# One of three output groups padded, scaling and decay powers open to GpSimd, the last output rows in two banks and two queues, and a new instruction table

## The chip, the core and the metric

The kernel runs on one core of a Trainium2 chip. The metric is the device time of one execution in microseconds (us). The core's engines work at the same time and wait for one another through semaphores: TensorE (PE in the rows, its weight loads PEld), VectorE (DVE), ScalarE (ACT), GpSimd (POOL), and SyncE (SP), which issues the DMA transfers.

## What is computed

```
# attention: r, k, v (4, 8, 768, 48); w, u (8, 48)
for t in range(S):
    cur = einsum('bhd,bhe->bhde', u * kt, vt)
    y[:, :, t] = einsum('bhd,bhde->bhe', rt, state + cur)
    state = w * state + einsum('bhd,bhe->bhde', kt, vt)
# x (4, 768, 384): the eight heads side by side
h = maximum(x @ w_in, 0)                      # w_in (384, 1024)
conv = sum over k of conv_w[k] * h shifted by k - 1 along the sequence
out = (h * sigmoid(conv)) @ w_out             # w_out (1024, 384)
```

All inputs and the output are 32-bit floats, but the three FFN weights arrive as 64-bit floats, read as pairs of 32-bit words, and are converted on the chip.

## The kernel before

The sequence of 768 is cut into groups of 128 positions (two chunks of 64), six to a batch, 24 in all. The recurrence is done by chunks, for four pairs of heads at a time, the two heads of a pair on the upper and the lower half of the partitions. For each group `prep` (L366) loads K and R into KR and scales them by powers of the decay (line L198 in the rows, written `KR<-KR,TKR`), makes a token-major K (`kt`, for groups 0 to 3 on TensorE at L381), the diagonal QQ (`q`, L393) and spreads QQ into RS (L410, L415 or L418). TensorE then computes scores (`VA`, into psA), additions to the state (`VU`, into psU) and outputs (`VY`, into psY). `chain` (L492) masks the scores into RS with a predicated copy (L496) and carries the state: it fades the old state into SD (L489, on ScalarE L487) and adds the new one into SS (L510, L515). For groups 0, 1 and 2 the visits VA, VU and VY are apart and borrow idle banks; from group 3 on one visit `V` holds the scores and additions of one group and the outputs of the one before.

`split` (L519) brings an output into XT as a rounded part (ScalarE, L527) and a remainder (VectorE, L528). The FFN wants the 384 features as three blocks of 128 partitions, while four pairs of heads give four blocks of 96 used partitions. Two ways lead there. In a padded group (`g < PAD`, before: groups 0, 1 and 2) TensorE writes the fourth pair's features, in three parts of 16, directly under the other three pairs: this needs a copy of the fourth pair's V (VP, L405) and of its state (SPP, L503), and more matmuls. In the other groups all four pairs are written apart, and six DMA transfers from XT to XT (L539) move the fourth pair's rows, once for each half of a batch.

The FFN works on eight units of three groups (382 or 386 columns) and on eight blocks f of 128 hidden features. `first` (L542) does nine matmuls into one of two HP banks (L559) and the chain relu (L566), taps (L567, L570, L570), sigmoid (L573), gate (L574) and the split of the result into GH (L576) and GL (L198). `second` (L581) does three matmuls (L591) for each of the three output blocks m = 0, 1, 2 into PO0 to PO2; after f = 7 ScalarE scales PO into OS (L598) and SyncE stores it. The weights come in 16 pieces into three ST buffers (`convert`, L326 to L353).

Nothing is scheduled at run time: the functions number their operations as they are called, and the table ORDER (L42) lists the numbers in the order in which each engine gets them. A suffix a, d or p picks ScalarE, VectorE or GpSimd for an operation marked "any". SyncE has one queue, in that order, so that a transfer that waits holds back all behind it.

Of the kernel before, what the change touches and what calls it, by code (L numbers as in the profile page):

```python
# [37 lines left out]
LEAD, EARLY, APART, PAD = 5, NEED[0], 4, NEED[0]  # L38
# [4 lines left out]
28 17 0 8 12 15 10 1 16 4 21 14 9 5 29 11 20 2 23 18 22 45 13 26 35 37 19 3 33 46 39 34 52 36 57 84 40 58 83 30  # L43
41 66 31 61d 42 43 38 74 59 6 32 75 62 78d 47 79 48a 54d 60a 49 210 76 209 50 63 7 51d 86a 67 53 65d 85 80 64a
87 232 82p 216 90 68 69 231 70a 55 44 77d 56 71p 105 92 212a 72 106 88 211 94d 109d 238 91 213 102 93 214 110
73a 89d 217 215d 107 95 111 81a 218d 112p 234a 97d 278 114 219 108a 279 113d 233 115 100 128 98 235 96a 99p 220
129 117 239 221p 285 116 118a 240d 126 101 301 24 236 25 119 241 300 280 281d 127 133 120a 242 282 121a 243d
237d 142 157d 123 125 283 160d 103 132 151 122 152 136p 124 104 134 148 150 287a 149 286 158d 200 303a 325 288
302 284d 307 135a 304 289 326 222 155 201 131 156 202 130 305 203 332 137 306p 223 204 154 224 140 159 144p 138
205 225 290p 139a 141 206 226 177p 269 145 172 175 153 227 146a 178p 228 143 270 291 161p 271 147 179 309a 272  # L50
229 162 164p 308 273 328a 371 310 274 176 171 292 275 327 207 230d 377 316 293 329 173 334a 208d 370 168 165 294
333 166p 170 315 169 276 180p 395 314 317 167 174 311 163 313 184p 318 339 295 277p 330 182 319 296 181a 331p
320 297 335 338 191 312d 321 361 195d 258 372 322 198p 189 186 183 190 373a 340 185 196p 379a 433 187 386 298
188 193 378 362 194 396 363 299d 244 387 380 336 374 388 364 337p 375 389 384 249 257 376p 365 385 381 259 250
# [97 lines left out]
def rwkv_ffn_kernel(tc, krd, krt, vt, wd, ut, w_in, conv_w, w_out, out):  # L152
# [4 lines left out]
    with ExitStack() as ctx:  # L157
# [24 lines left out]
        def act(n):  # L182
            return 0.093 + n / 1200.0
# [538 lines left out]
```

## Time and profile before

| what | value |
| --- | --- |
| time, median of 3 runs | 295.63 us (295.6 to 296.38) |
| the profiled execution | 296.4 us, of it 294.5 us span |
| TensorE busy | 281.9 us (96%) |
| VectorE, ScalarE, GpSimd busy | 245.8, 199.4, 102.4 us |
| weighted TensorE clock | 0.988 of 2.4 GHz |
| DMA moved | 37.48 MB |

The span runs from the first to the last instruction of the profiled execution; 1.9 us of its time lie outside. A busy share is an average over the whole span; what a stage waits for is read in that stage.

### The profile page before, as it was taken

To read this page: it belongs to the slowest core of one execution; us is meant where nothing else is said; L and a number is where in the kernel's file an instruction comes from. 1 tells how busy PE (TensorE), PEld (TensorE's weight loads), DVE (VectorE), ACT (ScalarE), POOL (GpSimd) and SP (SyncE) were. 2 spreads that over 40 slices of the span, in tenths; PEclk is the share of its full clock that TensorE was granted. 3 is DMA by queue.
4 is the path that set the end of the run, shared out by engine and by line. 5 is a ranking of instruction groups with operands and counts; after the bars stand their busy time and mean duration, and the time that the engine had idled before them with its cause. 6 is when DMAs were issued, how large, how long until landed. Compare 5 with 4: busy or idle time off the path is not lost.

```text
span 294.5 us, 10667 instructions
## 1 busy us (share of the span) xinstructions
PE 281.9 (96%) x4484; PEld 268.9 (91%) x4484; DVE 245.8 (83%) x469; ACT 199.4 (68%) x495; POOL 102.4 (35%) x134
## 2 busy tenths in 40 slices
PE   8798997899999999999999999999999999999995
PEld 3798886799999999999989999999999999999995
DVE  5889898989989799999988889989987866665771
ACT  4449798889886687764584568855665666567662
POOL 4121284353774722436384224334250014011100
PEclk9869999999999999999999999999999999999999
DMA  6969998695245664557266155561631002200202
GB/s 178 235 196 243 232 230 208 165 246 130 77 138 172 145 171 131 185 146 202 57 181 192 33 134 133 158 149 34 161 83 57 0 2 63 61 0 0 82 0 81
DMA packets 18499, 37.48 MB, mean 127 GB/s; under 512 B 3538, under 2 KB 11156, under 8 KB 18452
## 3 DMA queue, kind: packets, MB, share of 16 engines
q1 hardware_dynamic: 18452, 36.81, 47.1%
q8 instruction: 35, 0.57, 0.9%
q14 instruction: 12, 0.10, 0.1%
HBM read 30.01 MB, written 4.72 MB: 118 GB/s over the span
## 4 chain that ended last, share of the span: by engine, by line
PE 86%; DMA 6%; issue 2%; DVE 2%; POOL 1%; ACT 1%; SPq 0%; POOLq 0%
PE PO L591 35%; PE HP L559 33%; PE psY L479 9%; DMA ST<-in_w_in_dram 4%; PE psA L479 3%; PE psU L479 3%; DMA KR<-in_krd_dram 2%; PE PO L263 1%; PE HP L479 1%; PE PO L393 1%; POOL GL L198 1%; DVE KR L198 1%; SPq L202 0%; DVE KP L198 0%; ACT CC L336 0%
## 5 line engine op out<-in xcount | busy, mean ns | idle before, releaser
L559 PE MATMUL HP<-XT,wi 128*128 128x384 f32 (+1 forms) x576 | 111.7, 341 | 2.4 <-DVE GL L198 1.7
L591 PE MATMUL PO<-GH,wo 128*128 128x386 f32 (+1 forms) x384 | 109.8, 342 | 0.2 <-issue 0.2
L559 PEld LDWEIGHTS HP<-XT,wi 128*128 128x128 f32 x576 | 101.8, 188 | 3.6 <-DVE GL L198 1.8
L570 DVE SCALAR_TENSOR_TENSOR CV<-HP,cw,CV 128x382 f32<-128x382 f32 (+1 forms) x128 | 78.1, 614 | 16.9 <-ACT CV L567 15.2
L591 PEld LDWEIGHTS PO<-GH,wo 128*128 128x128 f32 x384 | 70.8, 189 | 1.6 <-issue 0.4
L591 PE MATMUL PO<-GL,wo 128*128 128x382 f32 (+1 forms) x192 | 65.1, 339 | 0.1
L198 POOL TENSOR_TENSOR GL<-SG,GH 128x382 fp32r<-128x382 f32 (+1 forms) x27 | 27.5, 1019 | 84.2 <-ACT GH L576 78.2
L566 ACT ACTIVATE HP<-HP 128x384 f32<-128x384 f32 (+1 forms) x64 | 30.6, 478 | 31.3 <-PE HP L559 30.9
L573 ACT ACTIVATE SG<-CV 128x382 f32<-128x382 f32 (+1 forms) x64 | 33.5, 524 | 26.1 <-DVE CV L570 25.5
L574 DVE TENSOR_TENSOR SG<-HP,SG 128x382 f32<-128x382 f32 (+1 forms) x64 | 35.4, 553 | 12.2 <-ACT SG L573 11.4
L479 PE MATMUL psY<-RS,KV 64*48 64x64 f32 x720 | 43.8, 221 | 1.3 <-issue 1.3
L479 PE MATMUL psY<-KR,SS 48*48 48x64 f32 x660 | 40.4, 216 | 0.5 <-issue 0.5
L576 ACT CAST GH<-SG 128x382 fp32r<-128x382 f32 (+1 forms) x64 | 32.5, 509 | 10.0 <-DVE SG L574 9.7
L567 ACT ACTIVATE CV<-HP,cw 128x382 f32<-128x382 f32 (+1 forms) x64 | 37.2, 581 | 1.4
L591 PEld LDWEIGHTS PO<-GL,wo 128*128 128x128 f32 x192 | 36.2, 189 | 0.4 <-POOL GL L198 0.4
L479 PEld LDWEIGHTS psY<-RS,KV 64*48 64x48 f32 x720 | 32.5, 121 | 1.6 <-issue 1.4
L198 DVE TENSOR_TENSOR KR<-KR,TKR 112x512 f32<-112x512 f32 x48 | 32.6, 691 | 0.8 <-DMA KR<-in_krd_dram 0.5
L479 PEld LDWEIGHTS psY<-KR,SS 48*48 48x48 f32 x660 | 30.8, 120 | 0.6 <-issue 0.6
L479 PEld LDWEIGHTS psA<-KR 48*64 48x64 f32 x704 | 22.3, 135 | 5.0 <-issue 3.2
L479 PE MATMUL psA<-KR 48*64 48x64 f32 x704 | 25.2, 221 | 0.0
L198 DVE TENSOR_TENSOR GL<-SG,GH 128x386 fp32r<-128x386 f32 (+1 forms) x37 | 20.5, 556 | 4.0 <-ACT GH L576 3.9
L479 PE MATMUL psU<-KV 64*48 64x48 f32 x672 | 20.1, 208 | 1.9 <-issue 1.8
(113 smaller groups left out, 347.4 us busy)
## 6 DMA issues: line engine op xcount, KB each, us to landing
KR<-in_krd_dram SPq DMA_DIRECT2D x24, 448.0 KB, 5.2
KV<-in_krt_dram SPq DMA_DIRECT2D x40, 192.0 KB, 3.7
KV<-in_vt_dram SPq DMA_DIRECT2D x48, 96.0 KB, 3.5
ST<-in_w_in_dram SPq DMA_DIRECT2D x16, 192.0 KB, 4.9
ST<-in_w_out_dram SPq DMA_DIRECT2D x8, 384.0 KB, 7.0
out_dram<-OS SPq DMA_DIRECT2D x12, 193.0 KB, 2.1
out_dram<-OS SPq DMA_DIRECT2D x12, 191.0 KB, 2.2
XT<-XT SPq DMA_DIRECT2D x42, 48.0 KB, 2.8
```

The lines of the kernel that those rows point to most:

```text
L198: op(eng, d, rd, wr, lambda e: e.tensor_tensor(**kw), cls, port=True)
L263: PE.matmul((psY, psU, HP[1], PO[0], PO[2])[min(k, 4)], wz[:, :128], wz, start=True, stop=True)
L393: PE.matmul(qb[o:o + 64, n:n + 1], kp[o:o + 48, p, t], uw[o:o + 48, p:p + 1], start=True, stop=True)
L479: PE.matmul(y, a, b_, start=s0, stop=s1)
L559: PE.matmul(hp, wi[a][:, j, fs], X[:, x, j, t], start=(j == 0 and k == 0), stop=(j == 2 and k == 2))
L566: op("act", 0.093 + n / 1200.0, [], [H_], lambda e: A.activation(hp, hp, AF.Relu, scale=1.0 / WS))
L567: op("act", 0.158 + n / 1200.0, [H_, "cw"], [("T", ti)], lambda e: A.activation(t1, hp[:, 1:n + 1], AF.Copy, scale=cw[:, 3 * f + 1:3 * f + ...
L570: op("dve", 0.117 + n * 1.085e-3, [H_, "cw"], [("T", ti)], lambda e, k=k: V.scalar_tensor_tensor(out=t1, in0=hp[:, k:n + k], scalar=cw[:, ...
L573: op("act", 0.11 + n / 1200.0, [("T", ti), "sgt"], [("SG", ti)], lambda e: A.activation(sg, t1, AF.Sigmoid))
L574: op("dve", dps(n), [H_], [("SG", ti)], lambda e: V.tensor_tensor(out=sg, in0=hp[:, 1:n + 1], in1=sg, op=ALU.mult), "GG")
L576: op("act", act(n), [("SG", ti)], [("GH", gi)], lambda e: A.copy(gh, sg))
L591: PE.matmul(PO[m][:, :n], wo[a][:, f, ms], g2[x], start=(f == 0 and k == 0), stop=(f == NF - 1 and k == 2))
```

## The change

Only group 2 is padded (`PADS = (2,)`). Groups 0 and 1 write their fourth pair apart, and six more XT to XT transfers, of 256 columns, move it after group 1's split; the first `first` reads what they bring. Their VP and SPP copies go, and the zeros for VP1 and SPP1 are written later. The scaling of K and R, the higher decay powers (PW2) and the diagonal decay matrix DW may go to GpSimd: of the 48 scalings 25 go there. In the last unit the output block m = 2 is summed as 192 columns in PO2 and 194 in psY, for all eight f; the output copies may go to VectorE (10 of 25 do), and the last store is issued by ScalarE's queue. A matmul of 256 columns on zeros (an `f` in the table) is put once between the first small matmuls. The table is new as a whole, so that engines and places change throughout.

```diff
@@ the constants @@
-LEAD, EARLY, APART, PAD = 5, NEED[0], 4, NEED[0]
+LEAD, EARLY, APART = 5, NEED[0], 4
+PADS = (2,)
@@ ORDER: the whole table is new; its first and its last line @@
-28 17 0 8 12 15 10 1 16 4 21 14 9 5 29 11 20 2 23 18 22 45 13 26 35 37 19 3 33 46 39 34 52 36 57 84 40 58 83 30
...
-1468 1453 1464 1472 1454d 1465 1471 1466d 1475 1482 1474 1483 1479 1484 1473 1480 1476 1481 1477 1478
+28 27 0 8 25 24 11 10 1 18 12 4 9 45 29 46 5 35 33 37p 79 52 17 36 20 2 39 19 58d 34 80 30 38p 57d 40 42 32 f
...
+1494a 1495
@@ powers2 @@
-            grow(32, 32)
-            grow(64, 31)
+            for n, m in ((32, 32), (64, 31)):
+                e.tensor_tensor(out=PW[:, :, n + 1:n + m + 1], in0=PW[:, :, 1:m + 1],
+                                in1=PW[:, :, n:n + 1].broadcast_to([112, NP, m]), op=ALU.mult)
@@ PW2 and DW @@
-        op("dve", 0.55, ["PW"], ["PW2"], powers2)
-        op("dve", 0.25, ["PW", "PW2", "ident"], ["DW"], lambda e: V.tensor_tensor(
+        op("any", {"dve": 0.55, "pool": 0.85}, ["PW"], ["PW2"], powers2, port=True)
+        op("any", {"dve": 0.25, "pool": 0.55}, ["PW", "PW2", "ident"], ["DW"], lambda e: e.tensor_tensor(
@@ prep @@
-                tt("dve", 512, ks, [(key, i)], "KR", out=v, in0=v, in1=W.unsqueeze(2).broadcast_to([112, NP, 2, C]), op=ALU.mult)
+                tt("any", 512, ks, [(key, i)], "KR", out=v, in0=v, in1=W.unsqueeze(2).broadcast_to([112, NP, 2, C]), op=ALU.mult)
...
-            if g < PAD:
+            if g in PADS:
@@ outputs @@
-                for p in range(3 if g < PAD else NP):
+                for p in range(3 if g in PADS else NP):
-                        if g < PAD:
+                        if g in PADS:
-                        if g < PAD and inter:
+                        if g in PADS and inter:
-                        mms.append((ps[64 - o:112 - o, m:m + C], KV[i][o:o + 64, 2, p, c, :], RS[j][o:o + 64, 2 * p + c, :], g >= PAD, not inter))
+                        mms.append((ps[64 - o:112 - o, m:m + C], KV[i][o:o + 64, 2, p, c, :], RS[j][o:o + 64, 2 * p + c, :], g not in PADS, not inter))
-            if g < PAD:
+            if g in PADS:
@@ chain @@
-                if g + (1 - c) < PAD:
+                if g + (1 - c) in PADS:
@@ split @@
-            r, np_ = (128, 3) if g < PAD else (112, NP)
+            r, np_ = (128, 3) if g in PADS else (112, NP)
-            if gi + 1 not in cuts or g < PAD:
+            if g in PADS or gi + 1 not in cuts and g + 1 not in PADS:
-            h = cuts.index(gi + 1) - 1
+            h = sum(c <= gi for c in cuts) - 1
@@ second @@
-            for m in range(NM):
-                ms = slice(m * 128, m * 128 + 128)
-
-                def mm(e, m=m, ms=ms):
+            h = n // 4 * 2
+            for m, x0, x1, bank, key in ((0, 0, n, PO[0], "o0"), (1, 0, n, PO[1], "o1")) + (
+                    ((2, 0, n, PO[2], "o2"),) if u < NU - 1 else ((2, 0, h, PO[2], "o2"), (2, h, n, psY, "psY"))):
+                ms, w_ = slice(m * 128, m * 128 + 128), x1 - x0
+
+                def mm(e, m=m, ms=ms, x0=x0, x1=x1, bank=bank):
-                        PE.matmul(PO[m][:, :n], wo[a][:, f, ms], g2[x], start=(f == 0 and k == 0),
+                        PE.matmul(bank[:, :x1 - x0], wo[a][:, f, ms], g2[x][:, x0:x1], start=(f == 0 and k == 0),
-                op("pe", 3 * n * 0.459e-3, [("wo", 0, f), ("wo", 1, f), ("GH", gi), ("GL", gi)], [f"o{m}"], mm, "f2", 3 * n)
+                op("pe", 3 * w_ * 0.459e-3, [("wo", 0, f), ("wo", 1, f), ("GH", gi), ("GL", gi)], [key], mm, "f2", 3 * w_)
-                    o = OS[q][:, :n]
-                    op("act", act(n), [f"o{m}"], [("OS", q)], lambda e, m=m, o=o: A.activation(
-                        o, PO[m][:, :n], AF.Copy, scale=1.0 / WS))
-                    dma([("OS", q)], [("out", u, m)], out[ms, b * S + t0:b * S + t0 + n], o, 128, 4 * n, cls="out")
+                    o = OS[q][:, :w_]
+
+                    def store(e, bank=bank, o=o, w_=w_):
+                        if e is A:
+                            A.activation(o, bank[:, :w_], AF.Copy, scale=1.0 / WS)
+                        else:
+                            V.tensor_scalar(out=o, in0=bank[:, :w_], scalar1=1.0 / WS, scalar2=None, op0=ALU.mult)
+                    op("any", {"act": act(w_), "dve": dps(w_)}, [key], [("OS", q)], lambda e, st=store: st(e))
+                    last = key == "psY"
+                    dma([("OS", q)], [("out", u, m, x0)], out[ms, b * S + t0 + x0:b * S + t0 + x1], o, 128, 4 * w_,
+                        0.6 if last else 0.52, cls="out", eng="act" if last else "sp")
```

TensorE, groups 0 and 1 (matmuls grouped as in the program; HP_108, HP_109, PO_110, PO_111 are the borrowed banks HP0, HP1, PO0, PO1, and KV_64 to KV_66 the buffers of groups 0 to 2). Before:

```order
L479 MATMUL psU<-KV_64 48x48 x16
L479 MATMUL HP_108<-KR_62 64x64 x16
L479 MATMUL psY<-RS_67,VP_120 64x64 x2
L479 MATMUL psY<-RS_67,KV_64 48x64 x2
...
L479 MATMUL HP_109<-KV_65 48x48 x16
L393 MATMUL PO_111<-uw,KP_117 64x1 x16
L381 MATMUL psU<-DW,KR_63 64x48 x16
L479 MATMUL PO_111<-KR_63 64x64 x16
L479 MATMUL psU<-KV_66 48x48 x16
L479 MATMUL PO_110<-RS_68,VP_121 64x64 x2
L479 MATMUL PO_110<-KR_62,SPP_123 64x64 x2
```

The same place with the change:

```order
L483 MATMUL psU<-KV_64 48x48 x16
L483 MATMUL HP_108<-KR_62 64x64 x16
L483 MATMUL HP_109<-KV_65 48x48 x16
L483 MATMUL psY<-RS_67,KV_64 48x64 x10
L483 MATMUL psY<-KR_61,SS_71 48x64 x2
...
L385 MATMUL psU<-DW,KR_63 64x48 x16
L397 MATMUL PO_111<-uw,KP_117 64x1 x16
L483 MATMUL PO_110<-RS_68,KV_65 48x64 x2
L483 MATMUL PO_110<-KR_62,SS_72 48x64 x2
...
L483 MATMUL PO_111<-KR_63 64x64 x16
L483 MATMUL psU<-KV_66 48x48 x16
```

Group 0's output (into psY) now stands behind group 1's additions (HP_109) and has lost its VP and SPP matmuls; group 1's output (into PO_110) has lost them too and stands ahead of group 2's scores and additions instead of behind them.

SyncE, the transfers around the reload of the K and R buffers (KR_61, KR_62, KR_63) and of the stores' new place. Before:

```order
L202 DMA KR_61<-in_krd_dram 112x1024
L202 DMA ST_97<-in_w_in_dram 64x768 x2
L202 DMA KV_65<-in_krt_dram 64x768 x2
L202 DMA ST_98<-in_w_out_dram 128x768
L202 DMA uu<-in_ut_dram 64x192
L202 DMA ST_96<-in_w_in_dram 64x768 x2
L202 DMA uu<-in_ut_dram 64x192
L202 DMA KR_62<-in_krd_dram 112x1024
L202 DMA KV_64<-in_vt_dram 64x384
```

With the change:

```order
L205 DMA KR_61<-in_krd_dram 112x1024
L205 DMA KV_64<-in_vt_dram 64x384
L205 DMA ST_96<-in_w_in_dram 64x768 x2
L205 DMA ST_97<-in_w_in_dram 64x768 x2
L205 DMA ST_98<-in_w_out_dram 128x768
L205 DMA XT_75<-XT_75 16x2x256 x6
L205 DMA KR_62<-in_krd_dram 112x1024
L205 DMA KV_64<-in_vt_dram 64x384
L205 DMA ST_96<-in_w_out_dram 128x768
```

Six transfers of XT to XT, which wait for group 1's split, now stand ahead of group 4's K and R (KR_62) and of the second half of group 3's V (KV_64).

## Rows read from the trace of the kernel before

**Rows 1.** The page's head and its first part (span, busy time of each engine), and the row of its third part on the fetching of instructions (packets, MB, share of the 16 DMA engines).
```profile
span 294.5 us, 10667 instructions
PE 281.9 (96%) x4484; PEld 268.9 (91%) x4484; DVE 245.8 (83%) x469; ACT 199.4 (68%) x495; POOL 102.4 (35%) x134
q8 instruction: 35, 0.57, 0.9%
```

**Rows 2.** Busy time by stretch: from and to in us, the length, then for PE, PEld (weight loads), DVE, ACT and POOL the busy us and the instructions, then TensorE's granted clock as a share of 2.4 GHz, the DMA share, GB/s.
```profile
14.00:16.00 2.00, 0.79 (x19) 0.78 (x20) 2.00 (x4) 0.00 (x0) 0.93 (x2) 0.50 0.82 227
18.00:20.00 2.00, 2.00 (x48) 2.00 (x46) 2.00 (x6) 0.72 (x3) 0.00 (x0) 0.58 0.44 111
...
60.00:100.00 40.00, 40.00 (x642) 38.65 (x633) 36.92 (x70) 32.38 (x89) 25.71 (x30) 1.00 0.58 156
100.00:140.00 40.00, 39.67 (x772) 37.58 (x771) 37.98 (x71) 28.43 (x76) 15.48 (x19) 1.00 0.57 157
140.00:180.00 40.00, 39.53 (x671) 38.12 (x670) 35.54 (x68) 25.37 (x61) 15.94 (x17) 1.00 0.40 111
```

**Rows 3.** The same view, cut at TensorE's four longest gaps: the four stretches of work, and the first and the last of the gaps, which lie between them (columns as in rows 2).
```profile
0.00:13.46 13.46, 11.92 (x221) 8.22 (x222) 9.54 (x25) 6.18 (x17) 3.60 (x19) 0.98 0.84 205
13.46:15.21 1.75, 0.00 (x1) 0.00 (x0) 1.72 (x4) 0.00 (x0) 1.47 (x2) 0.50 0.73 205
15.21:27.50 12.29, 12.29 (x382) 12.20 (x381) 10.43 (x23) 8.12 (x25) 2.59 (x6) 0.82 0.78 216
...
28.59:45.65 17.06, 15.85 (x381) 14.52 (x381) 15.92 (x33) 14.48 (x40) 8.21 (x9) 1.00 0.99 227
...
47.36:53.20 5.84, 5.83 (x126) 5.49 (x127) 5.06 (x11) 5.02 (x16) 3.96 (x5) 1.00 0.90 224
53.20:54.49 1.29, 0.00 (x0) 0.00 (x0) 1.28 (x4) 0.99 (x3) 0.58 (x1) 1.00 0.82 221
```

**Rows 4.** TensorE in order of time: start, us, line, operation, output and inputs, shapes, how many, and in brackets the idle time before and what ended it. Of group 0's and group 1's outputs and the first FFN matmuls.
```profile
19.17 0.42 PE L479 MATMUL psY<-KR,SS 48*48 48x64 f32 x4
19.39 0.42 PE L479 MATMUL psY<-RS,VP 64*64 64x64 f32 x4
...
24.35 0.27 PE L479 MATMUL PO<-RS,VP 64*64 64x64 f32 x2
...
26.01 0.28 PE L479 MATMUL PO<-RS,KV 64*48 64x64 f32 x4
26.13 0.28 PE L479 MATMUL PO<-KR,SS 48*48 48x64 f32 x4
...
32.82 3.41 PE L559 MATMUL HP<-XT,wi 128*128 128x384 f32 x18
39.48 1.85 PE L559 MATMUL HP<-XT,wi 128*128 128x384 f32 x9 [0.52 <-DVE SG L574]
```

**Rows 5.** VectorE and ScalarE in order of time (columns as in rows 4), before 50 us: the predicated copy into RS, the two halves of a split into XT, and ScalarE's forms of the diagonal and of the fading.
```profile
19.35 0.73 DVE L496 COPY_PREDICATED RS<-mask,HP 128x512 f32<-128x512 int32 x1
47.82 0.68 DVE L528 TENSOR_TENSOR XT<-psY,XT 112x512 fp32r<-112x512 f32 x1
46.99 0.57 ACT L527 CAST XT<-psY 112x512 fp32r<-112x512 f32 x1
38.44 2.00 ACT L415 ACTIVATE RS<-eye,QQ 128x64 f32<-128x64 f32 x8
40.77 1.00 ACT L487 ACTIVATE SD<-SS,PW 112x48 f32<-112x48 f32 x4
```

**Rows 6.** SyncE's stores from XT to XT (the moves between partitions): issue time in ns min/median/max and how many, then us from issue to landing, over the whole span; and how long the loads issued from 26 to 32 us took to land (how many, KB each, median us).
```profile
L202 SPq DMA_DIRECT2D XT<-XT x42: 585/614/1759, 62.7 to 251.4; - x42
DMA to landing us min/median/max: 2.1/2.8/5.4
KV<-in_vt_dram SPq DMA_DIRECT2D x2, 96.0 KB, 6.1
uu<-in_ut_dram SPq DMA_DIRECT2D x1, 48.0 KB, 5.0
```

**Rows 7.** GpSimd's and VectorE's groups by line and shape: how many | busy us, mean ns of one | idle before them; and in order of time a row of GpSimd, and two of the same operation on VectorE, the second of which lies over GpSimd's.
```profile
L198 POOL TENSOR_TENSOR KP<-KR 112x512 f32<-112x512 f32 x1 | 1.3, 1285 | 5.4 <-DVE KR L198 5.4
L198 DVE TENSOR_TENSOR KR<-KR,TKR 112x512 f32<-112x512 f32 x48 | 32.6, 691 | 0.8 <-DMA KR<-in_krd_dram 0.5
77.56 1.02 POOL L198 TENSOR_TENSOR KV<-KV 128x384 f32<-128x384 f32 x1
21.77 0.35 DVE L489 TENSOR_TENSOR SD<-SS,PW 112x192 f32<-112x192 f32 x1
77.10 1.70 DVE L489 TENSOR_TENSOR SD<-SS,PW 112x192 f32<-112x192 f32 x1
```

**Rows 8.** The end, in order of time (columns as in rows 4), and the page's row on the landing of output stores.
```profile
285.87 0.34 PE L591 MATMUL PO<-GL,wo 128*128 128x386 f32 x1
286.41 0.34 PE L591 MATMUL PO<-GL,wo 128*128 128x386 f32 x1
...
290.84 0.34 PE L591 MATMUL PO<-GH,wo 128*128 128x386 f32 x1
291.22 0.49 ACT L598 ACTIVATE OS<-PO 128x386 f32<-128x386 f32 x1 [0.57 <-PE PO L591]
out_dram<-OS SPq DMA_DIRECT2D x12, 193.0 KB, 2.1
```

More of the change, by code (lines that the diff above doesn't have):

```diff
@@ new lines @@
+495 508 450 511 496 407a 349 420p 497 509a 405 451p 498 512 499 421p 513 506a 514 523 462 413 423p 515 411 414
+406 516 419p 483 521 408 417 517 409a 522 507 422 418p 555 503a 410 412 524 518 463d 525 520 500 467 526 556
+501p 527 557 469d 528 488p 558 533 473 481 470 534 559 519p 482 471a 532 474 484 564 489p 560 529 485 566 561
+545 530 567 472 424a 510 490 491d 478 531d 416 565 486d 475 562 577 550p 568 479 563d 607 569 544 578 492a 468
+477 597 551p 570 476 571 480 576 553d 598 504 608 487d 599 606 549d 572 619 600 592p 618 573 535 552 537p 601
@@ new lines @@
+702d 695 723 731 712 706 696p 703 743 711 707 732 675 704p 724 644 714p 705 725 753 774 726 733 645 741 719d 734
+754 773 713d 727 764 701 728p 735 746p 736 775 757p 765 759d 785 737 766 744 767 762p 738 768 776 747 815 769
+758d 739 752 748d 740p 755 770 787 749 816 777 745 786 771 821p 756 778 797 669 750 788 760p 779 780 772d 799
+802d 789 820p 841 781 761 798 790 751 838 763p 791 835 782 800 792 842d 793 824d 783 794 784p 826 803 814 795
+804d 806 796p 836d 844 805 827 807 819p 828 801 813 870a 829 853 877 883p 855 845 830 868 846 822d 831 823 832
@@ new lines @@
+969a 967 1043 984p 979 959 1006 983 971 960 950p 1000 1007a 972 1003 961 1051p 1001a 1009 962d 992 993 970 985p
+994 1018 1010 1049d 1020 1011 1032 995 1033 1012 996 1035a 997 1050 998 1013 1030 1086 999p 1021 1014 982 1039
+1015 1045 990p 1040 976 1062 1036 1022 1041 1037d 1053 1004a 1047p 977 1023 1038 1044 1034 1079a 1087 1064 1046d
+978 1054 1019 1024 1055 1031 1002 1025 975 1063 1052d 1026 1077 1008 1016 1027 974 1017p 1056 1028 973 1057
+1092p 1065 1029d 1083 1089 1058 1088 1059 1148 1093p 1075 1084 1066 1085 1074 1080 1149 1067 1154d 1106 1081a
@@ new lines @@
+1068 1076 1090d 1108 1060 1094 1097 1061p 1069 1078 1070 1091p 1095d 1107 1098 1118 1099 1082 1120 1152p 1100
+1133 1101 1071 1102 1103 1109 1147 1096d 1104 1005 1072 1135d 1105p 1211d 1121 1110 1073d 1111 1112 1132 1122
+1113 1119 1139 1134 1209p 1130 1123 1131 1114 1124 1174 1115 1155p 1168 1136 1116 1125 1171 1137p 1159 1126
+1117p 1172a 1127 1138 1128 1175d 1203p 1177 1169a 1153d 1160 1157p 1161 1140 1187 1178 1214p 1186 1162 1143 1188
+1210p 1163 1141 1201 1129d 1170 1164 1179 1150 1165 1145 1180 1200 1144 1207 1181 1189 1151 1182 1173 1183 1146
@@ new lines @@
+1156 1198 1176 1190 1199 1158d 1166 1142 1184 1216 1167p 1191 1192 1185p 1226 1193 1212p 1225 1204 1194 1208
+1227 1205a 1195 1239 1202 1217 1238 1213 1228 1218 1206 1242d 1219 1240 1220 1229 1221 1196 1222 1230 1197p 1237
+1223 1231 1244 1246 1224p 1232 1233 1215p 1257 1234 1247 1243 1255 1248 1256 1235 1249 1258 1236p 1250 1251 1269
+1252 1259 1268 1245 1260 1280 1253 1261 1270 1254p 1262 1263 1281 1264 1271 1267 1241 1272 1291 1273 1274 1282
+1292 1275 1293 1276 1265 1294 1309 1266p 1295 1296 1277 1297 1303 1310 1278p 1279 1311 1306 1304a 1312 1321
```

91 lines of the change are left out of this document (34 added, 57 removed).

## The prediction

> **What bounds the kernel now.** I read the page's first part, then the busy time by stretch, then TensorE in order of time. TensorE is busy for 281.9 of 294.5 us [rows 1], and from 60 to 180 us it lacks only 0.33 + 0.47 us [rows 2]: there nothing but fewer matmuls would help, VectorE (37.98 of 40 us in the second of these stretches) runs close behind it, and a new order can mostly lose. What can be won lies in the first 55 us and behind the last matmul.
>
> The first 55 us have three losses. *Gaps.* TensorE stands still four times: from 13.46 to 15.21, 27.50 to 28.59, 45.65 to 47.36 and 53.20 to 54.49 us, 5.84 us in all [rows 3]. The stretches between hold 382, 381 and 126 matmuls, close to three, three and one times 128, wherever in a visit that falls. Each matmul has its weight load, so 128 of them are 256 instructions, and the 35 packets and 0.57 MB of the fetching row [rows 1] are 16 KB each; 2 x 4484 instructions over 35 packets are 256 a packet. I read the gaps as waits for the next packet of the program while the DMA engines are busy (0.73 and 0.82 in the two gaps shown). *Clock.* In the stretch from 14 to 16 us the granted clock is 0.50, that is 1.2 of 2.4 GHz, and still low in part from 18 to 20 [rows 2]: four small matmuls take 0.22 us there, against 0.12 later [rows 4]. It was 0.98 in the mean up to 13.46 [rows 3] and fell after the single-column `q` matmuls. *Order.* The FFN's first matmul starts at 32.82 us, behind three groups, and its third piece waits 0.52 us for VectorE [rows 4].
>
> At the end the last matmul starts at 290.84, its copy runs from 291.22 to 291.71, and a store of 193 KB lands 2.1 us after issue [rows 8].
>
> **The change part by part.**
>
> *Less padding.* Group 0 goes from 36 to 24 matmuls and group 1 from 48 to 32; each 32-bit matmul runs as two instructions, so 56 fewer. Group 0's ran at 0.22/4 = 0.055 us, group 1's at 0.12/4 = 0.03: 24 x 0.055 + 32 x 0.03 = 2.3 us of TensorE. This is a gain only if nothing else holds up the first FFN matmul, and now something does: six transfers.
>
> *The new path to 32.82 us.* Group 1's output began at 24.35 us [rows 4]. Ahead of it TensorE loses 1.3 us of group 0, and the 64 instructions of group 2's scores and additions (64 x 0.03 = 1.9 us) now come behind: 21.1 us as far as TensorE goes. But the diagonal (2.00 us) and a fading (1.00) for it go to ScalarE one behind the other, ahead of a predicated copy of 0.73 [rows 5]; I put its start at 22.2, an estimate between 21.1 and 24.35. Its 64 instructions end at 24.1; the rounded part takes 0.57 and the remainder 0.68 [rows 5], with some 0.6 us of other VectorE work ahead of the latter: 25.9. SyncE then issues six transfers at 0.61 each [rows 6], the last one at 25.9 + 5 x 0.61 = 29.0. A transfer of this kind lands after 2.8 us in the median and 5.4 at most, but these six are issued into the crowded stretch, where a load of only 48 KB took 5.0 [rows 6]. So the first FFN matmul can start between 29.0 + 2.8 = 31.8 and 29.0 + 5.4 = 34.4; I take the middle, 33.1, near the 5.0 of that stretch being half right. Group 2's own output, behind it on TensorE, is done by about 31 and does not decide. Against 32.82 that is +0.3 us (-1.0 to +1.6): the 2.3 us saved are spent before the FFN starts.
>
> SyncE is held by the first of the six until 25.9. Queued behind are group 4's K and R and the second half of group 3's V. That half is issued near 30.3 and lands 6.1 later [rows 6], at 36.4; group 3's additions come after two FFN pieces (33.1 + 3.4 + a `q` of 1 us = 37.5), so 1 us of cover is left; without it, the visit would wait by what it is late.
>
> *K and R, powers, fading on other engines.* One scaling takes 1.285 us on GpSimd (the row of KP has its shape) and 0.691 on VectorE [rows 7]; 25 move, 32 us onto an engine that is busy for 102.4 of 294.5 us and 17 us off VectorE [rows 1]. After 60 us that is worth nothing, since TensorE is full; its cover is that lead. Between 33 and 55 us VectorE gates the third FFN piece by 0.52 us [rows 4] and I count 0.5 as gained. Bounds: 0, and 0.8 with the 0.33 and 0.47 of the middle also gone; on the other side +1.0 if a scaling of 1.285 us comes late once for a visit.
>
> *Gaps.* 112 instructions fewer and two more shift the places of the gaps. The first stays within group 0's additions, at 221 matmuls; the second falls into waits for VectorE that are there anyway; of the last two, 3.0 us, the last's stretch now also holds FFN matmuls, which give a fetch more time. I take -0.8 us, between -3.0 (both gone) and +1.5 (one more gap like the rows' mean of 1.46).
>
> The Trainium skill (Runtime: NRT & Kernel Launch, section "Instruction fetch mechanics") says that instructions come in 16 KiB blocks of 256 and that crossing into one is mostly hidden. Block size and count agree with rows 1 and 3, the hiding does not where the DMA engines are full: by the page the gaps would be worth 0 and nothing of them could be won; by the rows they are 5.84 us.
>
> *Clock and the new matmul on zeros.* It takes at most 0.2 us in a wait. I take the low clock as unchanged, since the single-column matmuls stay; without it 2 us less, and if it lasted through group 1's and 2's outputs, 2 us more.
>
> *The end.* For the last unit, 24 matmuls become 48. Three of 386 columns take 0.54 us [rows 8], 0.18 each, of which 386 columns at 2.4 GHz are 0.161: 0.02 is fixed, so +0.5 us for 24 more (bounds 0 and +1.4, if a half takes as long as 0.06 beyond its columns). The copy of half the columns lasts perhaps 0.33 instead of 0.49 (-0.16), the store skips the hand-over to SyncE and is half as large (-0.2; 0 to -0.5 of its 2.1). Sum +0.1.
>
> **Sum.** +0.3 - 0.5 - 0.8 + 0.1 = -0.9 us, and -0.2, a quarter of what the middle lacks: -1.1. On the profiled execution's own 296.4 us (294.5 span and 1.9 around) that is 295.3. That execution lies at the upper edge of the three runs; the median is 295.63, and on it I forecast 294.5 us, 0.38% less. The measurement tells about 0.3% (0.9 us) from no change.
>
> **Rivals.**
>
> *The gain is hidden anyway.* The transfers land at the late end of the middle (33.6), the gaps keep their 5.84 us: +0.8 - 0.5 + 0.1 = +0.4, or 296.0. For it: the first 55 us are held by DMA and by several engines at once, so that a saved microsecond is waited out elsewhere. Against it: VectorE's wait at 39.48 is real and its load falls. Chance 0.30.
>
> *Slower: the six transfers.* They wait for group 1's remainder on VectorE, whose list is long, and stand in the queue behind four loads of 64x768 words and one of 128x768, 1.2 MB. If VectorE is 1.5 us later than I put it and they need 5.4 us, the first FFN matmul starts at 29.0 + 1.5 + 5.4 = 35.9, +3.1 us; with -0.5 and +0.1, and no gap won, 298.3. It decides from 34.1 on (+1.3 with -0.4 is +0.9). Chance 0.15.
>
> *Slower: VectorE held by GpSimd.* A fading on VectorE took 1.70 us while GpSimd ran back to back, the last of its operations ending at 78.58 [rows 7]; alone, at 21.77 us, it took 0.35. So it was held up, by 1.35 us. If each of the 25 scalings held VectorE for its whole 1.285 us, that is 32 us against 17 relieved: +15 us on an engine with 3.1, 2.0 and 4.5 us free in the three stretches of 40 [rows 2], so some +5 us that TensorE waits out, 300.6. Against it: the 48 scalings on VectorE have a mean of 0.691 with GpSimd busy beside them. Chance 0.04. The Trainium skill (SBUF — State Buffer, on the shared port pair) states this as a rule: an exclusive lock, held for a whole instruction, against VectorE operations with two SBUF inputs; the row of 77.10 agrees.
>
> **Chances.** My forecast 0.51 (its own range 292.4 to 294.7: the low end with both late gaps gone or the clock restored), hidden 0.30, slower 0.19. So faster by over 0.3% 0.51, within 0.3% 0.30, slower 0.19. The range 292.2 to 297.0 leaves out the worst slower cases and a gain beyond 3.4 us.
>
> **What would show it.** Right: the first FFN matmul (output HP, input XT and wi) near 33 us, waiting for a transfer from XT to XT; matmuls per stretch between gaps again near multiples of 128; no wait of the third FFN piece for VectorE; TensorE's idle time before 60 us some 1 us smaller and still under 1 us from 60 to 180; the last copy near 0.33 us. Wrong: an FFN start beyond 34.1 or before 31.8, a low clock after 20 us, or TensorE idle in the middle with GpSimd named as releaser.

## The result: 0.56% slower, and where the time went

The changed kernel takes 296.97 us in the median of 20 executions, the kernel before 295.5 us in 20 beside them: ratio 1.0056, 95% interval 1.0034 to 1.0078, some 1.6 us longer where 1.1 us less was forecast. Timed again with other kernels it was 1.0042 (1.0004 to 1.0079). The ratios leave out executions that a slower state of the chip lengthened. The profiled execution took 296.92 us. Its page (span; granted clock in 40 slices), and TensorE by stretch, as in [rows 2]:

```profile
span 295.2 us, 10633 instructions
...
PEclk9867999999999999999999999999999999999999
```

```profile
14.00:16.00 2.00, 1.79 (x35) 1.53 (x34) 2.00 (x3) 0.17 (x1) 1.78 (x2) 0.50 0.91 205
...
22.00:24.00 2.00, 1.89 (x60) 1.83 (x58) 1.79 (x5) 1.82 (x5) 0.51 (x1) 0.87 0.99 219
24.00:26.00 2.00, 2.00 (x43) 2.00 (x41) 1.72 (x5) 1.76 (x5) 0.00 (x0) 0.50 0.89 243
...
30.00:33.00 3.00, 2.92 (x102) 2.77 (x99) 2.71 (x7) 1.07 (x3) 1.36 (x1) 1.00 0.46 101
33.00:36.00 3.00, 2.01 (x23) 1.67 (x20) 2.59 (x6) 2.97 (x8) 0.12 (x1) 1.00 0.44 120
...
60.00:100.00 40.00, 40.00 (x674) 38.55 (x673) 37.60 (x72) 36.77 (x107) 25.66 (x26) 1.00 0.60 155
100.00:140.00 40.00, 40.00 (x777) 38.39 (x776) 36.29 (x70) 24.70 (x61) 21.36 (x23) 1.00 0.53 145
140.00:180.00 40.00, 40.00 (x673) 38.44 (x672) 36.89 (x69) 22.78 (x53) 23.16 (x23) 1.00 0.48 132
```

From 60 us on TensorE is full: the 0.33 + 0.47 us that it lacked from 100 to 180 us [rows 2] are gone. The second low clock (22 to 27 us) is new, and so are the DMA shares of 0.46 and 0.44 between 30 and 36 us. TensorE in order of time, and its waits by what ended them (us in total, times, longest), against [rows 3, 4]:

```profile
23.54 0.45 PE L483 MATMUL PO<-RS,KV 64*48 64x64 f32 x4
...
34.42 2.08 PE L563 MATMUL HP<-XT,wi 128*128 128x384 f32 x9 [0.99 <-DMA XT<-XT]
37.46 1.84 PE L563 MATMUL HP<-XT,wi 128*128 128x384 f32 x9
41.96 1.84 PE L563 MATMUL HP<-XT,wi 128*128 128x384 f32 x9 [0.86 <-DVE SG L578]
44.48 1.85 PE L563 MATMUL HP<-XT,wi 128*128 128x384 f32 x9 [0.68 <-DVE SG L578]
...
70.11 3.36 PE L563 MATMUL HP<-XT,wi 128*128 128x388 f32 x18
```

```profile
PE HP L563 <- DVE SG L578: 2.8, 4, 0.9
...
PE psY L483 <- issue: 0.2, 1, 0.2
```

The gaps that the prediction read as waits for the program are nearly gone (0.2 us of 5.84; the profile calls such a wait "issue"). The first FFN matmul starts at 34.42 instead of 32.82 us. A piece is the nine matmuls of one `first`, and the gate is VectorE's product SG (L578): four waits for it make 2.8 us instead of 0.69. The second unit starts at 70.11 instead of 69.25; from there to the end of the span it is 225.09 us, before 225.25. SyncE's queue and ScalarE show why the DMA engines stood half idle:

```profile
26.35 0.53 SPq L205 DMA_DIRECT2D ST<-in_w_out_dram  x1
28.49 5.00 SPq L205 DMA_DIRECT2D XT<-XT  x6
33.60 0.51 SPq L205 DMA_DIRECT2D KR<-in_krd_dram  x1
```

```profile
31.93 0.55 ACT L340 ACTIVATE CC<-ST 128x384 f32<-128x384 f32 x1 [3.65 <-DMA ST<-in_w_in_dram]
...
33.72 0.46 ACT L531 CAST XT<-psY 128x384 fp32r<-128x384 f32 x1
```

Six early XT transfers take 5.00 us to issue, 0.83 each in the mean, not the 0.61 of [rows 6]: most take about that, the longest 1.52. The load of group 4's K and R behind them goes out at 33.60, where SyncE of before issued it at 28.98. ScalarE's copy of group 2's sums into XT ends only 0.24 us ahead of the first FFN matmul: two things could gate it. VectorE then waits for those K and R:

```profile
37.84 1.74 DVE L201 TENSOR_TENSOR KR<-KR,TKR 112x512 f32<-112x512 f32 x2 [0.86 <-DMA KR<-in_krd_dram]
```

Two taps follow it without a pause, then ScalarE's sigmoid and the gate (41.35 to 41.91), for which TensorE waits 0.86 us at 41.96: the first of the four waits goes back to the late load. The other three are not traced so. And the end, against [rows 8]:

```profile
281.72 0.28 PE L597 MATMUL psY<-GH,wo 128*128 128x194 f32 x1
281.83 0.27 PE L597 MATMUL PO<-GH,wo 128*128 128x192 f32 x1
281.94 0.28 PE L597 MATMUL PO<-GL,wo 128*128 128x192 f32 x1
...
291.79 0.27 PE L597 MATMUL psY<-GH,wo 128*128 128x194 f32 x1
```

Halves start 0.11 us apart, whole ones 0.177: a pair costs 0.047 us more than a whole one, 24 pairs 1.1 us. Behind the last matmul's start 3.4 us remain instead of 3.66.

### The profile page after: what moved, and what is told of

Same layout as the page of the kernel before. It is cut to its first block, busy times and chain, and to the rows that moved or that the text cites. A ratio compares the mean times of both kernels' runs of the same rounds, so it can differ in the third digit from the quotient of the medians.

```text
span 295.2 us, 10633 instructions
## 1 busy us (share of the span) xinstructions
PE 285.0 (97%) x4453; PEld 271.0 (92%) x4453; DVE 243.3 (82%) x453; ACT 195.1 (66%) x481; POOL 140.3 (48%) x155
## 4 chain that ended last, share of the span: by engine, by line
PE 87%; DMA 6%; SPq 3%; DVE 2%; issue 1%; ACT 0%; ACTq 0%
PE HP L563 34%; PE PO L597 34%; PE psY L483 9%; PE psA L483 3%; PE psU L483 3%; SPq L205 3%; DMA KV<-in_vt_dram 2%; DMA KV<-in_krt_dram 2%; DMA XT<-XT 1%; PE PO L483 1%; PE HP L483 1%; PE psY L597 1%; DVE TT L350 1%; DVE CV L574 0%; PE psU L385 0%
## 5 line engine op out<-in xcount | busy, mean ns | idle before, releaser
L563 PE MATMUL HP<-XT,wi 128*128 128x384 f32 (+1 forms) x576 | 113.0, 342 | 3.7 <-DVE SG L578 2.8
L597 PE MATMUL PO<-GH,wo 128*128 128x382 f32 (+2 forms) x384 | 107.1, 338 | 0.0
L201 POOL TENSOR_TENSOR GL<-SG,GH 128x382 fp32r<-128x382 f32 (+1 forms) x36 | 37.9, 1060 | 93.2 <-ACT GH L580 87.3
L578 DVE TENSOR_TENSOR SG<-HP,SG 128x382 f32<-128x382 f32 (+1 forms) x64 | 35.4, 553 | 12.4 <-ACT SG L577 11.5
L483 PE MATMUL psY<-RS,KV 64*48 64x64 f32 x728 | 42.7, 220 | 0.0
L483 PE MATMUL psY<-KR,SS 48*48 48x64 f32 x664 | 39.8, 215 | 0.2 <-issue 0.2
L580 ACT CAST GH<-SG 128x386 fp32r<-128x386 f32 (+1 forms) x64 | 31.8, 508 | 9.2 <-DVE SG L578 9.2
L201 POOL TENSOR_TENSOR KR<-KR,TKR 112x512 f32<-112x512 f32 x25 | 34.0, 1365 | 6.3 <-DMA KR<-in_krd_dram 6.1
L201 DVE TENSOR_TENSOR KR<-KR,TKR 112x512 f32<-112x512 f32 x23 | 20.0, 885 | 1.4 <-DMA KR<-in_krd_dram 1.4
```

Source lines behind the costliest of these rows:

```text
L201: op(eng, d, rd, wr, lambda e: e.tensor_tensor(**kw), cls, port=True)
L483: PE.matmul(y, a, b_, start=s0, stop=s1)
L563: PE.matmul(hp, wi[a][:, j, fs], X[:, x, j, t], start=(j == 0 and k == 0), stop=(j == 2 and k == 2))
L578: op("dve", dps(n), [H_], [("SG", ti)], lambda e: V.tensor_tensor(out=sg, in0=hp[:, 1:n + 1], in1=sg, op=ALU.mult), "GG")
L580: op("act", act(n), [("SG", ti)], [("GH", gi)], lambda e: A.copy(gh, sg))
L597: PE.matmul(bank[:, :x1 - x0], wo[a][:, f, ms], g2[x][:, x0:x1], start=(f == 0 and k == 0), stop=(f == NF - 1 and k == 2))
```

## Experiments

Ratios are to the kernel before, with 95% intervals. Kernels that start with "a" are edits of the changed kernel, with "b" of the kernel before (in the changed code, its own order). In the expectations VY1 are group 1's outputs, the bonus products are `q`, and a low part is the remainder that VectorE puts into XT. The theories: A, the six early XT transfers gate the FFN and hold SyncE's queue; B, TensorE's clock falls a second time; C, scalings on GpSimd make VectorE late; D, the end costs; O, the written order costs; E, later, ScalarE's copy gates the FFN.

**1. Which part costs, by undoing or adding one.**

[a_krdve] K and R scalings back on VectorE: in ORDER `-100p`, `+100` and so for all 25.

> The changed kernel with all 48 K and R scalings back on VectorE, everything else as changed. Theory C (the scalings on GpSimd make VectorE late): the four waits of the first FFN matmuls for VectorE's gate product, 2.77 us in the changed kernel, shrink to under 1 us, and the time falls by 1.5 to 2.5 us, to 294.5 to 295.5 us. Theory A (the six early XT transfers gate the first FFN matmul and hold SyncE's queue) and theory B (TensorE's clock falls a second time because it has less to do): the first FFN matmul stays at 34.2 to 34.6 us and the time within 0.5 us of 297.0, or longer, since VectorE takes back 25 scalings of 0.69 us.

The ratio is 1.0348 (1.0268 to 1.0429), 8.6 us slower than the changed kernel. In its profile (309.05 us, one of the longer of its six executions) TensorE's waits for the gate are 9.1 us, nine times. The scalings on GpSimd help this order, so theory C falls.

[b_krpool] The same 25, the powers and the decay matrix on GpSimd, in before's order.

> The kernel before in its own order and with its padding, with those 25 K and R scalings, the second half of the powers and the decay matrix on GpSimd that the change has there; nothing else changed. Theory C: the waits for VectorE's gate before the first FFN matmuls grow from 0.69 us to over 2 us and the time is 1 to 2.5 us longer, 296.5 to 298 us; the scalings left on VectorE take longer each than the 691 ns of before. Theories A and B: within 0.5 us of before, 295.0 to 296.0 us.

The ratio is 1.006 (1.0025 to 1.0095). But not by theory C: the waits for the gate are 0.6 us in two, the scalings on VectorE last 730 ns, those on GpSimd 1470:

```profile
PE psU L482 <- issue: 3.4, 2, 2.6
PE psY L482 <- issue: 1.9, 2, 1.5
PE psA L482 <- POOL KR L200: 1.5, 1, 1.5
...
PE HP L562 <- issue: 1.1, 1, 1.1
```

There is one wait of 1.5 us for a scaling on GpSimd, in an order not made for it, and gaps in the code, as before.

[a_pads012] Groups 0, 1 and 2 padded: `-PADS = (2,)`, `+PADS = (0, 1, 2)`, the six XT transfers out of ORDER and the VP and SPP copies back in.

> The changed kernel's order with groups 0, 1 and 2 padded as before, so without the six early XT transfers. Theory A: the first FFN matmul starts by 33.5 us instead of 34.42, the load of KR that SyncE issued at 33.60 us goes out before 30 us, the waits for VectorE's gate shrink with it, and the time falls by 1.0 to 1.6 us, to 295.4 to 296.0 us. Theory B: the second stretch at 0.50 of the clock (24 to 26 us) is gone, VY1 takes 2 us again instead of 3.6, but TensorE has 2.3 us more to do before it, so the first FFN matmul stays at 34.0 to 34.6 us. Theory C: 296.5 to 297.5 us, the waits for the gate unchanged.

The ratio is 1.0112 (1.0049 to 1.0174): not faster. Without any early XT transfer the first FFN matmul still starts at 34.10, behind ScalarE's copy:

```profile
30.12 0.27 PE L483 MATMUL psY<-KR,SPP 48*64 48x64 f32 x2 [1.44 <-issue]
34.10 0.44 PE L563 MATMUL HP<-XT,wi 128*128 128x384 f32 x1 [0.37 <-ACT XT L531]
```

The low clock from 22 us on is gone, but a gap in the code is back, and so is the padding (2.3 us by the prediction). So theory A can't stand as put: the transfers aren't the only gate, and taking them out whole does not bring the time back.

[b_pads2] Group 2 alone padded, in before's order.

> The kernel before in its own order, with group 2 alone padded and the six XT transfers put in right behind group 1's low part; nothing else changed. Theory A: the first FFN matmul moves from 32.8 to between 33.8 and 34.6 us, SyncE's next loads go out 3 to 5 us later, and the time is 0.8 to 1.8 us longer, 296.3 to 297.3 us. Theory B: a second stretch at 0.50 of the clock shows between 20 and 28 us, and VY1 takes 3 us or more. Theory C: 2.3 us of padding matmuls saved and nothing lost, 293.5 to 295.5 us.

The ratio is 1.014 (1.0086 to 1.0193), slower than any theory said: group 1's remainder comes late in VectorE's old order (31.43 us), and the transfers with it.

```profile
37.49 4.80 PE L562 MATMUL HP<-XT,wi 128*128 128x384 f32 x18 [4.63 <-DMA XT<-XT]
```

[b_tail] The end alone, in before's order.

> The kernel before with the end alone changed: the last unit's third block of rows summed in two banks, copied in two halves and stored by two queues, in the changed kernel's order from the last unit's fifth piece on. If the end costs something (theory D: 24 more matmuls of half the width): the last matmul starts 0.3 to 0.9 us later and the span is 0.2 to 0.7 us longer, 295.7 to 296.2 us. If the shorter end pays for them: the stretch behind the last matmul's start falls from 3.66 to 3.4 us or less and the time is 295.0 to 295.6 us. Theories A, B, C: no change beyond 0.3 us.

The ratio is 1.0082 (1.0047 to 1.0116). That is theory D, and more: beside the 1.1 us of halves its TensorE waits at 285 to 287 us, since ORDER puts pieces sooner than ScalarE and VectorE finish them, and the last matmul starts 33.7 us after the last unit's first, against 31.3 before. Its profile also has a gap in the code of 2.05 us near 29 us, 1.0 us longer than before's there, so not all of the 2.4 us is the end's.

[b_all] All three parts in before's order.

> All three parts of the change (padding of group 2 alone, scalings and decays on GpSimd as in the change, the end in two banks) put into the order of the kernel before, so that only the written order differs from the changed kernel. If the three parts cost the time (A, C, D): as slow as the changed kernel or slower, 296.5 to 299 us, since nothing in this order was moved to suit them. If the written order itself costs it (theory O: the same work in another order): 294.0 to 295.5 us, at or below before.

The ratio is 1.0319 (1.0259 to 1.038). Theory O falls as put: with these parts the old order is 7.8 us slower than the changed kernel's. Nothing in it was moved to suit them, so this does not say what a better order would give.

**2. The clock.** [a_fill] `+f f f` ahead of the first `q`, `+f f f f` ahead of the second and of group 2's outputs.

> The changed kernel with eleven more 256-column matmuls of zeros into a bank that nothing reads, at places where TensorE waits: three ahead of the first bonus products (10.2 us), four ahead of the second (12.6 us), four ahead of group 2's outputs (29.2 us). Theory B: the granted clock between 14 and 28 us rises, VY1 takes 2 us instead of 3.6, the first FFN matmul starts 1 to 2 us earlier than 34.42 us and the time falls to 295 to 296 us. Theories A and C: the clock rises or not, the first FFN matmul stays at 34.2 to 35.0 us, and the time is within 0.7 us of 297.0 us.

The ratio is 1.0081 (1.0045 to 1.0118). In the profile the second low stretch is gone (clock 1.00 from 20 us on), and the first FFN matmul starts at 34.44, as in the changed kernel. Theory B falls as the cause of the late start: what TensorE does sooner, it waits out.

```profile
24.00:26.00 2.00, 1.81 (x69) 1.84 (x71) 2.00 (x6) 2.00 (x6) 0.00 (x0) 1.00 0.95 272
```

```profile
34.44 1.91 PE L563 MATMUL HP<-XT,wi 128*128 128x384 f32 x9 [1.48 <-DMA XT<-XT]
```

It does not fall as a cause of the time. The profiled execution (295.7 us) is one of the shortest of twelve with a median of 298.0, and their mean granted clock, 0.980, is no higher than the changed kernel's 0.981: the added matmuls did not keep the clock up in most of them.

**3. The transfers' queue.** [a_xm2q] Three of the six on ScalarE's queue:

```
-  32, (gi + 1 - cuts[h]) * 512, 0.6, "XM")
+  32, (gi + 1 - cuts[h]) * 512, 0.6, "XM", eng="act" if g == 1 and o else "sp")
```

> The changed kernel with three of the six early XT transfers issued on ScalarE's queue and three on SyncE's. Theory A: the last issue ends at 31.0 instead of 33.5 us, the first FFN matmul starts at 33.3 to 33.6 us (it then waits for group 2's low part), SyncE's next load of KR goes out at 31 us, and the time falls by 0.8 to 1.5 us, to 295.5 to 296.2 us. Theories B and C: the first FFN matmul comes up to 1 us earlier, but the waits behind it (for VectorE's gate) grow by as much and the time stays within 0.4 us of 297.0 us.

The ratio is 0.9984 (0.995 to 1.0017): 2.1 us less than the changed kernel.

```profile
27.16 2.51 SPq L205 DMA_DIRECT2D XT<-XT  x3
30.91 0.33 SPq L205 DMA_DIRECT2D KR<-in_krd_dram  x1
```

```profile
33.19 0.44 PE L563 MATMUL HP<-XT,wi 128*128 128x384 f32 x1 [0.39 <-ACT XT L531]
...
42.35 1.84 PE L563 MATMUL HP<-XT,wi 128*128 128x384 f32 x9 [0.52 <-DVE SG L578]
...
67.46 3.36 PE L563 MATMUL HP<-XT,wi 128*128 128x388 f32 x18
```

The first FFN matmul gains 1.23 us (the other eight of its piece start at 33.78), the second unit 2.65.

[a_hold] The same, and three transfers of this size into a buffer `DU` that nobody reads, on SyncE behind its own three: `+dma(ks, [("DU", k)], DU[k][48:64], F[16 * k:16 * k + 16, :, 3, tu], 32, 1024, 0.6, "DU")`.

> The kernel with the six early XT transfers on two queues, and in addition three transfers of the same size into a buffer that nobody reads, on SyncE's queue right behind its own three. The first FFN matmul then has its rows as early as on two queues, but SyncE's next loads go out about 2.5 us later, at 33 us. If the whole gain of the two queues came from the first FFN matmul's earlier start: as on two queues, 294.0 to 295.2 us. If it came from the loads behind the transfers: the first FFN matmul stays at 33.2 to 33.6 us, but the waits for VectorE's gate come back (over 2 us before the pieces 2 to 5) and the time is 296 to 297 us.

The ratio is 1.0067 (1.0039 to 1.0094): the whole gain is gone.

```profile
31.54 2.66 SPq L205 DMA_DIRECT2D DU<-XT  x3
34.31 0.51 SPq L205 DMA_DIRECT2D KR<-in_krd_dram  x1
```

```profile
33.98 3.38 PE L568 MATMUL HP<-XT,wi 128*128 128x384 f32 x9 [1.21 <-DMA XT<-XT]
...
42.57 1.84 PE L568 MATMUL HP<-XT,wi 128*128 128x384 f32 x9 [0.61 <-DVE SG L583]
46.36 2.36 PE L568 MATMUL HP<-XT,wi 128*128 128x384 f32 x9 [1.95 <-DVE SG L583]
```

The first FFN matmul is 0.8 us later than on two queues (0.2 us by the other eight), the fourth piece 4.0 us; between 30 and 60 us VectorE waits 1.9 us for K and R and 1.4 us for the columns of the next group, neither of which shows in [a_xm2q]. The clock is 0.63 from 33 to 36 us as well, so this one profile doesn't part the late loads from the clock. The executions do: of those behind the ratios with a mean clock of 0.981 to 0.983, four of [a_hold] take 297.4 us in the mean, the kernel before beside them 295.6; six of [a_xm2q] take 294.7, the kernel before beside them 295.5. So the held queue costs 2.6 us at the same clock, about the 2.5 us by which the two ratios differ.

**4. The first FFN matmul itself** (theory E: it waits for ScalarE's copy, which the new order puts behind four conversions that wait for weights). [b_xhlate] in before's order on ScalarE:

```
+ACTIVATE TT, CC, TT, CC <-ST
 CAST XT<-psY
-ACTIVATE TT, CC, TT, CC <-ST
```

> The kernel before with the same copy moved the other way: behind the four weight conversions that follow it on ScalarE, as in the changed kernel; nothing else changed. Theory E: the copy starts at 33.6 to 34.2 us instead of 31.43, the first FFN matmul at 34.2 to 35.0 us instead of 32.82, and the time is 0.8 to 1.8 us longer, 1.003 to 1.006 of before, as much as the change cost. If a later first FFN matmul is made up further on: 0.998 to 1.002 of before.

The ratio is 1.0002 (0.9961 to 1.0042). The copy moved to 34.41 and the first FFN matmul by 2.2 us, and nothing came of it; the second unit starts at 69.09, before at 69.25.

```profile
34.41 0.48 ACT L530 CAST XT<-psY 128x384 fp32r<-128x384 f32 x1
```

```profile
35.05 3.74 PE L562 MATMUL HP<-XT,wi 128*128 128x384 f32 x18
...
69.09 3.50 PE L562 MATMUL HP<-XT,wi 128*128 128x388 f32 x18
```

[a_xh] The copy in the changed kernel ahead of two of its four conversions.

> The changed kernel with one instruction moved: ScalarE copies group 2's sums into XT behind two of the four weight conversions that stand ahead of that copy, instead of behind all four. Theory E (the first FFN matmul waits for that copy, which stands behind conversions that wait for weights in ScalarE's order): the copy starts at 32.8 instead of 33.7 us, the first FFN matmul at 33.4 to 34.0 us instead of 34.42, and the time falls by 0.3 to 1.0 us, to 1.001 to 1.004 of before. Theory A (the XT transfers gate it): the first FFN matmul stays at 34.2 to 34.6 us behind XT, and the time at 1.004 to 1.007 of before.

The ratio is 1.0015 (0.9974 to 1.0057), which can't be told from the changed kernel's. The first matmul moves to 33.29, but alone: the other eight of its piece now wait for VectorE's remainder and start later than the nine did in the changed kernel.

```profile
33.29 0.41 PE L563 MATMUL HP<-XT,wi 128*128 128x384 f32 x1 [1.43 <-DMA XT<-XT]
34.85 2.93 PE L563 MATMUL HP<-XT,wi 128*128 128x384 f32 x8 [1.15 <-DVE XT L532]
```

[a_xm2q_xh] With two queues also:

> The changed kernel with the six early XT transfers on two queues and the copy moved as in the first kernel of this call. If both gate (A and E): the copy starts near 31.8 us instead of 32.66, the first FFN matmul at 32.3 to 32.7 us instead of 33.19, and the time is 0.994 to 0.997 of before. If the copy does not matter once the transfers are early: 0.998 of before as with two queues alone.

The ratio is 1.0011 (0.9974 to 1.0048): the first FFN matmul is at 31.55, the earliest of all, the other eight at 32.91, and there is no gain over two queues alone.

```profile
31.55 0.41 PE L563 MATMUL HP<-XT,wi 128*128 128x384 f32 x1 [0.26 <-ACT CC L340]
32.91 2.93 PE L563 MATMUL HP<-XT,wi 128*128 128x384 f32 x8 [0.96 <-DVE XT L532]
```

By [b_xhlate] theory E falls as a price. The other two, in which one matmul moved and not the piece, test it less than their starts suggest; they show that the first FFN matmul is no measure of the time.

**5. The end, and the best.** [a_end1] `-(2, 0, h, PO[2], "o2"), (2, h, n, psY, "psY")`, the last copies and stores as before.

> The changed kernel with the end of before: the last unit's third block of rows summed in one bank again, its copies on ScalarE, all stores on SyncE's queue, in before's order. Theory D (the end costs): halves are spaced 0.111 us and whole matmuls 0.177 us in the changed kernel's trace, so 24 pairs cost 1.1 us and the shorter stretch behind the last matmul gives 0.26 us back; without the change of the end the time falls by 0.6 to 1.2 us, to 295.8 to 296.4 us, and the last matmul starts at 290.7 us instead of 291.8. If the end is no cost: 296.7 to 297.3 us.

The ratio is 1.0027 (0.9986 to 1.0068); the changed kernel beside it ([after_again]) has 1.0042. [a_xm2q_end1] With two queues too:

> Both repairs together: the six early XT transfers on two queues and the end of before. If the two costs add (1.0056 for the change, 0.9984 with two queues, 0.8 us for the end): 0.9945 to 0.9970 of before, 293.8 to 294.6 us, faster than both kernels. If the end is no cost: 0.998 of before.

The ratio is 0.9965 (0.9939 to 0.999), the first that is faster than before. [a_both_xh] With the moved copy:

> Three repairs together: early XT transfers on two queues, the copy moved, and the end of before. If the three add: 0.991 to 0.995 of before, 293.0 to 294.2 us, the fastest of all. If the copy's move adds nothing: 0.9965 of before as with the other two alone.

The ratio is 0.9941 (0.9898 to 0.9984). In all three pairs the end of before is the faster one (by 0.15, 0.19 and 0.70%), each within the intervals; TensorE's rows say 1.1 - 0.3 = 0.8 us, 0.3%. The profiles agree: from the second unit's start to the end of the span, three kernels with the end of before take 224.0 to 224.4 us, six with the changed end ([after], [after_again], [a_fill], [a_xm2q], [a_xh], [a_xm2q_xh]) 224.8 to 225.3; [a_hold], with 224.4, does not fit.

[after_again] The changed kernel once more:

> The changed kernel itself, unedited, timed beside the three others of this call. All theories: 1.003 to 1.008 of before, first FFN matmul at 34.0 to 34.8 us behind the XT transfers.

The ratio is 1.0042. Here the transfers were out by 31.13 us, and the first FFN matmul waited 1.9 us for ScalarE's copy; then the clock fell:

```profile
30.00:33.00 3.00, 1.69 (x64) 1.56 (x59) 1.21 (x4) 1.72 (x4) 1.34 (x1) 1.00 0.29 68
33.00:36.00 3.00, 2.29 (x7) 2.04 (x8) 2.89 (x7) 2.68 (x7) 0.00 (x0) 0.73 0.91 231
36.00:45.00 9.00, 9.00 (x109) 8.04 (x109) 4.94 (x11) 4.48 (x11) 3.27 (x4) 0.52 0.77 186
```

Group 4's K and R went out at 31.25 us here, at 33.60 in the first profile, at 30.91 in [a_xm2q] and at 31.59 in [a_both_xh], the fastest kernel of all. One profile shows one execution, and the issue of that load alone does not rank the kernels.

## Why the prediction was wrong

*The new path to 32.82 us* is the step that failed. It priced the six transfers by when the first FFN matmul can start (+0.3 us) and put what they hold up on SyncE's queue at nothing: it named the loads behind them and left 1 us of cover. The start came at 34.42, beyond the 34.1 from which the rival "six transfers" was to decide; its sign was right, but the start is not what costs: 2.2 us of it cost nothing in [b_xhlate]. The cost is the queue. Six issues took 5.0 us instead of 3.7, the DMA engines ran half empty behind them, and the next groups' loads came late for VectorE. Two queues take off 0.72% (1.0056 to 0.9984), with the end of before 0.62% (1.0027 to 0.9965), with the moved copy only 0.04%; three more transfers in the same queue put 0.83% back on. The mean of the three pairs is 0.46%, 1.4 us; if two queues take off just what the prediction left out, the term is +1.7 instead of +0.3. Why the third pair's ratios show nothing stays open: their intervals (0.4% either way) allow both, and in the profiles the second unit starts 2.1 us earlier on two queues in that pair too (70.18 to 68.06), as in the others (2.65 and 2.13).

That the start was off by only 1.3 us is luck. The prediction had the six begin at 25.9 us; they began at 28.49, since group 1's output started at 23.54 instead of 22.2 and ran in the second low clock. It also had the FFN wait for the last of the six; the last was issued at 32.0, such transfers landed after 3.3 us at the least, and the first matmul ran at 34.42. Group 2's own output, which was "not to decide", gates the first FFN matmul through ScalarE's copy in [after_again] and [a_xm2q].

*The end* was mis-sized: +0.5 for halves, measured +1.1 (the term's upper bound was +1.4); the copy and store gained 0.3, near the 0.36 forecast. That is +0.8 instead of +0.1.

With these two, the sum of -1.1 becomes -1.1 + 1.4 + 0.7 = +1.0 us; measured were +1.2 (1.0042) and +1.6 (1.0056). What is left is within the intervals, but the agreement is in part luck: the sum keeps four terms that came out otherwise, the gaps, VectorE, the clock and the middle, which gained 0.8 us and not 0.2.

*The gaps in the code* fell by 5.6 us, not 0.8, in the first profile; [after_again] has 1.0 us of them. (Of the 5.84 us the profile itself puts 1.66, ahead of the piece at 47.36, down to VectorE's GL.) The arithmetic by 128 matmuls held for their places before, but not as a forecast: they vanish in an order with other waits, and come back (1.44 us) with the padding. The Trainium skill (Runtime: NRT & Kernel Launch, section "Instruction fetch mechanics") calls the crossing into a new block mostly hidden: 0.2 us in the changed kernel agree, 7.3 us in [b_krpool] don't. The gain did not reach the end: the second unit starts 0.86 us later than before.

*The clock* "unchanged" was wrong: 12 to 28 us lost 5.1 us of full-speed time (each stretch's length by one minus its clock) against 3.4 before. It did not set the FFN's start ([a_fill]); but in [after_again], behind a wait of 1.9 us for that start, it stays near half up to 45 us, and the 20 executions of the changed kernel run from 294.7 us (mean clock 0.988) to 298.6 (0.970). Their mean clock is 0.981 (0.979 in the second timing), that of the kernel before, timed beside the edits, 0.982 to 0.985. So part of the loss goes with the clock, and how large a part is open: at mean clocks of 0.981 to 0.983 six executions of [after_again] take 296.3 us and sixteen of the kernel before beside them 295.6, 0.7 us apart where the ratio says 1.2.

*VectorE.* The -0.5 us came as +2.1 in the first profile. GpSimd holding VectorE (the rival at 300.6) is not the reason; [a_krdve] shows the reverse. Scalings on VectorE went from 691 to 885 ns, but they take 826 ns in [a_krdve] with none on GpSimd. Late loads are the reason for the first of the four waits; for the rest that is argued. On two queues the waits for the gate are 1.2 us in [a_xm2q] but 2.3 in [a_xm2q_end1], so this path from the queue to the time is not shown throughout.

*Less padding* as such worked as put: its 2.3 us were spent before the FFN starts.

## What to carry to other kernels

Price a transfer by what it holds in its queue, not only by when it lands: six small transfers between buffers took 5 us to issue, and ahead of prefetches they left the DMA engines under half busy for 6 us. A second engine's queue, for the cost of one argument, took off 0.7, 0.6 and 0.04% in three pairs. A later or earlier start of a stage is worth nothing until one has seen that the stage's end moves with it. Splitting a matmul to shorten a tail costs more than its columns once for every accumulation step, and saves in the tail only once.

## What had not been expected

A 2.2 us later start of the FFN was made up by the second unit. With TensorE's waits spread otherwise, 5.6 us of waiting for the program vanished although the program is hardly shorter (4453 for 4484 matmul records). A half of 194 columns is spaced 0.11 us against 0.081 of columns at 2.4 GHz, where 386 columns need 0.177 against 0.161: the part beyond the columns was 0.03 us there, not the 0.02 taken from the full width. Each half also has a weight load of its own, and the rows don't tell which of the two sets the 0.11.
